# A first layer issued in another sequence, and a last output written out in two column halves

## The chip, the cores and the metric

The kernel runs on one core of a Trainium2 chip. The metric is device time in microseconds (us) of one execution; the median of three runs before the change is 726.11 us (725.8 to 727.15).

The engines are named as the profile names them: PE (TensorE, matrix products; PEld is its weight load), DVE (VectorE), ACT (ScalarE), POOL (GpSimd), SP (SyncE, which here only issues DMAs). SPq and ACTq are the sequencers of SP and ACT when they issue a DMA.

## The reference, cut to what matters

```python
def _attn_ref(q, k, v, alpha):            # (4, 8, 768, 48): a gated linear recurrence over time
    for t in range(S):
        state = alpha[:, :, t, :, None] * state + np.einsum('bhd,bhe->bhde', k[:, :, t], v[:, :, t])
        y[:, :, t] = np.einsum('bhd,bhde->bhe', q[:, :, t], state)

def _moe_ref(x, w_in, w_out, g_ln):       # first layer: x is (3072, 384), d_ff 1024
    h = x @ w_in
    solu = h * softmax(h)
    ln = (solu - mean(solu)) / sqrt(var(solu) + 1e-6) * g_ln
    return ln @ w_out

def _moe2_ref(x, w_in, w_out):            # second layer, d_ff 2048
    h = x @ w_in
    return (h * np.cos(h)) @ w_out
```

## The kernel before, in words

The work has two stages. The first stage does the recurrence and the first layer together, in 24 chunks of 128 tokens. The second stage does the second layer, in 6 blocks of 512 tokens by 16 chunks of the hidden dimension.

**The first stage.** A chunk i loads a pack (q, k and the decay alpha, 128 partitions) and v. DVE scans alpha forwards (`S1`, line 251), inverts the totals (`S3`) and scans backwards (`S4`, line 262). The scans scale q and k: the q product is `QP` on POOL or `QV` on DVE (line 276), the k product `KR` on POOL or `KV` on DVE (line 271). PE turns k (`TR`), ACT copies the result out (`KT`), PE makes scores (`SC`, line 295), DVE masks them (`MV`), PE makes the state (`ST`, line 346), DVE adds it up (`SD`, two halves), PE makes the values (`VA`, line 327). ACT and DVE split these into a high and a low part (`XH`, `XL`). Then come the hidden products of three k slices (`HD i.0` to `HD i.2`, line 395, 18 matmuls in all), DVE's maximum (`SM`, line 401), ACT's exponential (`EX`), the normalisation, turns (`TU`, `TH`, `TL`) and the projection (`PR`, `PX`).

**The weights.** They arrive as float64 bit patterns and are turned into float32 on the chip. For a block n: `CL` loads it (SP), `C1` shifts the upper word (DVE, line 183), `C2` and `CA` make the lower word on ACT (lines 190, 194), an integer add puts them together: `CD` on POOL or `CV` on DVE (line 198). `WH` copies the high part (ACT, line 212), and `WL` (POOL) or `WV` (DVE, line 218) subtracts the rest. Blocks 0 to 5 are `w_in` (512 columns each), 6 to 9 `w_out` (768 columns), 10 to 25 the second layer's, which `WS` stores to memory for later.

**The order.** Each engine works its queue strictly in order. `PLAN` is a text of 1104 words; the program walks it and issues one operation per word, so the sequence of words is the sequence of each engine's queue. `UN` is a matmul pair on constant data, with no use but to keep PE at work; five of them (`WARM`) stand ahead of the plan. `LP` and `LQ` load the decay part and the q and k part of a pack, `LV` loads v, `LD` all of it, and `ID` loads the identity, the mask and the norm's weights; `BP`, `BQ` and `BC` are the same loads issued by ACT.

**Buffers that set the order.** Line 459 and its like take PSUM tiles from one ring of three, tag `rot`: `TR` takes two, `TU` two, `ST`, `PR` and `UN` one each, and a new owner waits until the readers of the old one are done. Raw `w_in` blocks use two buffers for even and two for odd blocks, so the third even or odd load waits until the first is converted.

**The end.** `out_end` (line 626) copies the three output slices of a block from PSUM with a factor of 2 and stores each. For the last block, slice 0 is copied by ACT and stored by SP; slices 1 and 2 (`late`) are copied by DVE and stored by ACT's queue.

Of the kernel before, what the change touches and what calls it, by code (L numbers as in the profile page):

```python
# [79 lines left out]
NO3 TU2 C110 O24 O34 PR0.1 QV8 XL6 HD5.0 TH2.0 HD5.1 S48 A44 S19 KR8 TH2.1 TL2.1 TL2.0 C210 MV7 HD5.2 SA7 S39 TU3  # L80
PX0.1 TH3.0 SM5 TH3.1 EX5 VA7 TL3.0 TL3.1 O15 SC8 TR8 XH7 SQ4 PR1.0 O25 PA4 O35 PW4 HD6.0 KT8 PB4 XL7 S49 A45 HD6.1
CA10 NO4 HD6.2 TU4 CD10 MV8 VA8 PX1.0 SQ5 LD10 S110 QV9 TH4.0 TH4.1 SM6 EX6 TL4.0 CL11 ST8 C111 PR1.1 O16 O26 S310 O36
KV9 PA5 C211 PW5 S410 PB5 XH8 A46 SQ6 SD8 QV10 NO5 PA6 XL8 PX1.1 HD7.0 CL12 SP8 CA11 LD11 HD7.1 HD7.2 TL4.1 TR9 SC9
KT9 KV10 SM7 EX7 TR10 KT10 ST9 MV9 S111 VA9 SC10 A17 S311 TU5 SD9 PR1.2 O27 WS10 XH9 PW6 O37 TH5.0 HD8.0 XL9 CD11 QP11
C112 O47 S411 SP9 LD12 HD8.1 MV10 KV11 C212 TL5.0 S112 CL13 TH5.1 HD8.2 PB6 SQ7 TL5.1 PA7 CA12 PX1.2 NO6 VA10 SM8 EX8
ST10 SC11 QP12 CD12 WS11 CL14 TU6 SD10 C113 O18 PW7 PR2.0 S312 XH10 O28 SP10 C213 LD13 O38 WS12 S412 PB7 NO7 TH6.1
HD9.0 CA13 PX2.0 TH6.0 XL10 C114 HD9.1 HD9.2 CD13 KR12 TL6.0 O48 TL6.1 SQ8 SM9 PR2.2 CL15 MV11 EX9 TR12 A19 S113 PX2.2
KT12 SC12 S313 TU7 O29 VA11 PA8 O39 XH11 LD14 PR2.1 TH7.0 HD10.0 QV13 A49 PW8 MV12 TL7.0 HD10.1 XL11 S114 HD10.2 S413
S314 C214 TH7.1 PB8 TL7.1 SQ9 VA12 ST12 CA14 LD15 KR13 NO8 WS13 SM10 QV14 SD12 CV14 PX2.1 EX10 SC13 O110 TU8 TH8.0
PR3.0 XH12 O210 O310 TH8.1 S414 S115 HD11.0 WS14 KV14 XL12 PA9 PX3.0 C215 TL8.0 A410 HD11.1 MV13 SQ10 S315 PA10 HD11.2  # L90
PW9 TL8.1 PB9 PR3.2 TR13 CA15 KT13 VA13 PX3.2 ST13 TR14 SM11 NO9 S415 PW10 SC14 QP15 C115 KT14 SD13 XH13 SA13 XL13 TU9
MV14 CD15 TH9.0 TH9.1 EX11 TL9.0 CL16 PR3.1 TL9.1 C216 LD16 VA14 ST14 C116 KV15 S116 SD14 CA16 CL17 PX3.1 QP16 O111
SA14 O211 SC15 TR15 PR4.0 O311 XH14 CD16 WS15 HD12.0 HD12.1 C217 CA17 C117 S316 PB10 LD17 O411 HD12.2 SQ11 PA11 KT15
S117 PW11 S416 XL14 MV15 KR16 VA15 PX4.0 ST15 CL18 SM12 WS16 CV17 NO10 EX12 SD15 SC16 S317 SP15 TU10 O112 O212 PR4.1
# [853 lines left out]
```

## Time and profile before

| | |
|---|---|
| median of three runs | 726.11 us (725.8 to 727.15) |
| the profiled execution | 727.55 us |
| its span, first to last instruction | 725.7 us |
| PE busy | 708.5 us, 98% of the span |
| DVE, ACT, POOL busy | 81%, 60%, 17% |
| mean granted TensorE clock | 0.992 of full |

PE's busy share is not its share of peak: matmuls overlap, and at half clock the same matmul is busy twice as long. The span and the time of the profiled execution differ by 1.85 us, which lie outside the first and last instruction. The execution that was profiled was 1.4 us above the median.

### The profile page before, as it was taken

The numbers are of one execution on the slowest core, as the hardware profiler recorded it, in microseconds if no ns is written. First come the engines' busy times: TensorE is split into PE (matmuls) and PEld (weight loads), VectorE is DVE, ScalarE is ACT, GpSimd is POOL, SyncE is SP. The second block draws the span as 40 slices with busy tenths as digits, with TensorE's granted clock in tenths as the row PEclk, the third lists the DMA queues.
The fourth block names the chain that finished last, engine by engine and source line by source line (L and its number), as shares of the span: only waits on it lengthen the run. The fifth ranks groups of instructions, "written<-read, shape, count | busy, mean of one in ns | idle before, by whom it ended". The sixth has DMA issues, their size and how long they took to land.

```text
span 725.7 us, 14521 instructions
## 1 busy us (share of the span) xinstructions
PE 708.5 (98%) x5866; PEld 597.4 (82%) x5866; DVE 586.2 (81%) x995; ACT 432.2 (60%) x768; POOL 119.8 (17%) x113
## 2 busy tenths in 40 slices
...
GB/s 310 286 200 114 66 215 245 146 140 270 195 142 134 242 39 72 31 37 78 97 138 1 155 70 51 65 124 51 37 142 63 46 100 138 43 88 131 110 44 47
DMA packets 28010, 85.36 MB, mean 118 GB/s; under 512 B 3104, under 2 KB 6304, under 8 KB 27936
## 3 DMA queue, kind: packets, MB, share of 16 engines
...
q8 instruction: 48, 0.79, 0.5%
...
HBM read 73.33 MB, written 11.01 MB: 116 GB/s over the span
## 4 chain that ended last, share of the span: by engine, by line
PE 89%; DVE 6%; DMA 2%; ACT 1%; issue 1%; POOL 0%; SPq 0%; DVEq 0%; POOLq 0%
PE ph L395 12%; PE o L622 9%; PE o L624 9%; PE o L623 9%; PE h L577 9%; PE h L576 9%; PE h L575 9%; PE po L484 5%; PE po L485 4%; PE po L486 4%; PE px L327 4%; PE pa L295 3%; DMA pk<-pack 2%; PE pl L463 1%; DVE P L251 1%; DVE c L401 1%
## 5 line engine op out<-in xcount | busy, mean ns | idle before, releaser
L595 ACT ACTIVATE g<-r,consts 128x512 f32<-128x512 f32 x96 | 69.6, 725 | 98.8 <-DVE r L589 98.8
L582 ACT ACTIVATE n<-h,consts 128x512 int32<-128x512 f32 x96 | 66.1, 688 | 81.1 <-PE h L577 81.1
L622 PE MATMUL o<-gh,w2h 128*128 128x512 f32 x288 | 112.4, 390 | 0.0
L624 PE MATMUL o<-gl,w2h 128*128 128x512 f32 x288 | 112.2, 390 | 0.0
L577 PE MATMUL h<-x2h,w2l 128*128 128x512 f32 x288 | 112.2, 390 | 0.0
L576 PE MATMUL h<-x2l,w2h 128*128 128x512 f32 x288 | 112.2, 390 | 0.0
L623 PE MATMUL o<-gh,w2l 128*128 128x512 f32 x288 | 112.2, 390 | 0.0
L575 PE MATMUL h<-x2h,w2h 128*128 128x512 f32 x288 | 112.2, 389 | 0.0
L588 DVE SCALAR_TENSOR_TENSOR r<-n,h 128x512 f32<-128x512 int32 x96 | 66.0, 688 | 31.1 <-ACT n L582 30.6
L600 DVE TENSOR_TENSOR g<-g,h 128x512 f32<-128x512 f32 x96 | 66.1, 689 | 25.5 <-ACT g L595 25.4
L484 PE MATMUL po<-lth,wout_h 128*128 128x256 f32 x288 | 83.0, 288 | 1.9 <-DVE S L362 1.0
L485 PE MATMUL po<-ltl,wout_h 128*128 128x256 f32 x288 | 80.6, 280 | 0.0
L486 PE MATMUL po<-lth,wout_l 128*128 128x256 f32 x288 | 80.4, 279 | 0.0
L589 DVE SCALAR_TENSOR_TENSOR r<-n,r 128x512 f32<-128x512 int32 x96 | 67.4, 702 | 3.3
L610 DVE TENSOR_TENSOR gl<-g,gh 128x512 fp32r<-128x512 f32 x96 | 65.7, 684 | 0.8 <-ACT gh L605 0.8
L624 PEld LDWEIGHTS o<-gl,w2h 128*128 128x128 f32 x288 | 54.1, 188 | 11.3 <-DVE gl L610 0.2
L622 PEld LDWEIGHTS o<-gh,w2h 128*128 128x128 f32 x288 | 54.1, 188 | 11.2 <-ACT x2T L490 0.2
L623 PEld LDWEIGHTS o<-gh,w2l 128*128 128x128 f32 x288 | 54.1, 188 | 11.2
L577 PEld LDWEIGHTS h<-x2h,w2l 128*128 128x128 f32 x288 | 54.1, 188 | 11.2
L576 PEld LDWEIGHTS h<-x2l,w2h 128*128 128x128 f32 x288 | 54.1, 188 | 11.2
L575 PEld LDWEIGHTS h<-x2h,w2h 128*128 128x128 f32 x288 | 54.1, 188 | 11.1
L605 ACT ACTIVATE gh<-g 128x512 fp32r<-128x512 f32 x96 | 59.9, 624 | 1.1 <-DVE g L600 0.8
(114 smaller groups left out, 1363.3 us busy)
## 6 DMA issues: line engine op xcount, KB each, us to landing
...
```

The costliest lines, as they stand in the source:

```text
L395: PE.matmul(ph[:, n * 512:(n + 1) * 512], xs[:, k, :], w[:, k, n * 512:(n + 1) * 512], start=k == 0 and xs is xh and w is win_h, stop=k == ...
L484: PE.matmul(po, wout_h[:, k, fs], lh[:, k, :], start=k == 0, stop=False)
L485: PE.matmul(po, wout_h[:, k, fs], ll[:, k, :], start=False, stop=False)
L486: PE.matmul(po, wout_l[:, k, fs], lh[:, k, :], start=False, stop=k == NF1 - 1)
L575: PE.matmul(ph, wh[:, ks], xh[:, k, :], start=k == 0, stop=False)
L576: PE.matmul(ph, wh[:, ks], xl[:, k, :], start=False, stop=False)
L577: PE.matmul(ph, wl[:, ks], xh[:, k, :], start=False, stop=k == KT - 1)
L589: V.scalar_tensor_tensor(out=r, in0=n, scalar=-C2, in1=r, op0=ALU.mult, op1=ALU.add)
L595: A.activation(g, r, AF.Sin, bias=halfpi)
L622: PE.matmul(po, wh[:, fs], gh, start=c == 0, stop=False)
L623: PE.matmul(po, wl[:, fs], gh, start=False, stop=False)
L624: PE.matmul(po, wh[:, fs], gl, start=False, stop=c == NF2 - 1)
```

## The change

The plan has the same set of steps in another sequence, from its first word to its last, and some steps change their engine. `out_end` changes for the last block: slices 1 and 2 are stored by SP, and the last slice is copied and stored in two halves of 256 columns, the first by ACT (copy and store), the second by DVE (copy) and SP (store).

How the steps differ by kind, counted over the whole plan, before and after: loads issued by ACT 3 and 0; integer adds on POOL (`CD`) 18 and 10, on DVE (`CV`) 8 and 16; q products on POOL (`QP`) 9 and 17, on DVE (`QV`) 15 and 7; k products on POOL 15 and 14, on DVE 9 and 10; residues on POOL (`WL`) 4 and 3, on DVE (`WV`) 6 and 7; small mean steps on DVE (`O4`) 13 and 9, on ACT (`A4`) 11 and 15; `UN` 7 and 7.

```diff
 PLAN = """
-UN1 LP0 CL1 BP1 UN1 LP2 S10 BQ0 BC3 C21 CL0 CA1 C23 ID S30 CA3 C20 C11 S40 S11 CA0 CL2 S12 S31 LQ1 KV0 S41 C22 C13 C10
-UN1 CV3 C12 CV0 LV0 TR0 CL6 KT0 LQ2 QP0 SC0 UN1 ST0 MV0 CA2 SD0 WH0 WV0 S32 CL4 CD1 QV1 WH1 VA0 S42 C16 WH3 CL5 KR1
-XH0 C26 CA6 WV1 XL0 C24 SC1 UN1 TR1 C25 C14 CA4 UN1 CA5 MV1 C15 LV1 CV4 HD0.0 CD2 WH2 LD3 KT1 VA1 ST1 CV5 LV2 S13 WL3
-WH4 WV2 CL7 S33 WH5 WV4 WV5 KR2 CD6 S43 C17 TR2 CL8 WH6 QP2 C27 KR3 HD0.1 XH1 SD1 SP1 KT2 HD0.2 SC2 CA7 SM0 TR3 CD7
-ST2 XL1 EX0 MV2 WL6 A10 O20 KT3 LD4 C28 O30 A40 WH7 SQ0 VA2 PA0 SD2 S14 UN1 HD1.0 HD1.1 C18 S34 CA8 PW0 XH2 QV3 HD1.2
-S44 SC3 QP4 SM1 PB0 XL2 EX1 SP2 ST3 CL9 CD8 A11 MV3 VA3 NO0 O21 KR4 O31 XH3 LD5 C29 TU0 HD2.0 TH0.0 HD2.1 A41 SD3
...
+LP0 LP1 S10 CL1 LQ0 S11 CL0 C21 S30 LP2 C11 LQ1 LV0 S40 ID CL2 QV0 S31 KV0 S41 CA1 C20 CV1 CL5 S12 C22 C10 KV1 CL3 SC0
+WH1 S32 LQ2 CL6 CA0 C12 UN1 TR0 S42 CA2 MV0 CD0 KT0 C13 WV1 CV2 UN1 C25 CL7 WH0 LV1 CL4 UN1 QV1 C23 TR1 VA0 CA5 WH2
+ST0 KV2 SC1 C26 C15 C16 KT1 XH0 CD5 CA3 UN1 CD3 MV1 WV0 SD0 ST1 C24 WH3 XL0 CA4 LD3 WH5 C14 SD1 TR2 UN1 QP2 KT2 WV2
+CA6 WV3 CV4 VA1 HD0.0 HD0.1 WH4 S13 SA1 XH1 CV6 WV4 S33 C27 LV2 WV5 S43 HD0.2 CL8 WH6 SC2 SM0 EX0 KR3 XL1 TR3 WL6 ST2
+MV2 A10 CA7 VA2 O20 KT3 O30 UN1 A40 SQ0 LD4 QP3 S14 PA0 HD1.0 XH2 C17 S34 S44 HD1.1 XL2 PW0 HD1.2 SD2 CD7 UN1 SM1 SC3
+SP2 C18 PB0 MV3 NO0 C28 QP4 EX1 KR4 O11 CA8 ST3 O21 TU0 TH0.0 VA3 LD5 O31 WH7 SD3 O41 SQ1 PA1 TH0.1 CD8 HD2.0 TL0.0
...
 """
...
                 ob = pools["q3"].tile([128, BLK], F32, name=f"ob{b}_{f}", tag="ob", bufs=3)
+                dst = a["outT"][f * 128:(f + 1) * 128, b * BLK:(b + 1) * BLK]
                 late = b == NBLK - 1 and f > 0
+                cut = BLK // 2 if late and f == KT - 1 else 0
+                if cut:
+                    A.activation(ob[:, :cut], O[b][f][:, :cut], AF.Copy, scale=2.0)
+                    A.dma_start(dst[:, :cut], ob[:, :cut])
                 if late:
-                    V.tensor_scalar(ob, O[b][f], 2.0, None, ALU.mult)
+                    V.tensor_scalar(ob[:, cut:], O[b][f][:, cut:], 2.0, None, ALU.mult)
                 else:
                     A.activation(ob, O[b][f], AF.Copy, scale=2.0)
-                (A if late else SP).dma_start(a["outT"][f * 128:(f + 1) * 128, b * BLK:(b + 1) * BLK], ob)
+                SP.dma_start(dst[:, cut:], ob[:, cut:])
```

## Rows read from the trace of the kernel before

**Rows 1.** The page: busy time of each engine, its share, its instructions.

```profile
PE 708.5 (98%) x5866; PEld 597.4 (82%) x5866; DVE 586.2 (81%) x995; ACT 432.2 (60%) x768; POOL 119.8 (17%) x113
```

**Rows 2.** One stretch: PE, PEld, DVE, ACT, POOL busy; clock; DMA share; GB/s.

```profile
40.00:60.00 20.00, 19.54 (x306) 15.51 (x305) 19.05 (x30) 17.44 (x36) 12.19 (x10) 1.00 0.53 176
```

**Rows 3.** Waits of PE, whole span: total us, times, longest.

```profile
PE pkt L286 <- DVE pk L271: 3.3, 1, 3.3
PE pa L295 <- DVE pk L276: 2.3, 1, 2.3
PE po L484 <- DVE S L362: 1.0, 1, 1.0
PE pa L295 <- POOL pk L271: 0.4, 1, 0.4
```

**Rows 4.** DVE's timeline of the head: start, us, line, operation.

```profile
4.63 1.23 DVE L251 TENSOR_TENSOR_SCAN P<-pk,d1p 128x516 f32<-128x516 f32 x1 [3.10 <-DMA pk<-pack]
6.94 0.43 DVE L183 TENSOR_SCALAR magso<-rawi 128x512 int32<-128x512 int32 x1 [0.80 <-DMA rawi<-win]
7.29 1.23 DVE L262 TENSOR_TENSOR_SCAN R<-pk,d1r 128x516 f32<-128x516 f32 x1
8.43 2.15 DVE L251 TENSOR_TENSOR_SCAN P<-pk,d1p 128x516 f32<-128x516 f32 x1
12.73 0.66 DVE L271 TENSOR_TENSOR pk<-pk,R 128x512 f32<-128x512 f32 x1
14.77 1.40 DVE L183 TENSOR_SCALAR mage<-rawi 128x512 int32<-128x512 int32 x1
19.62 1.68 DVE L218 TENSOR_TENSOR win_l<-mage,win_h 128x512 fp32r<-128x512 f32 x1
35.65 1.22 DVE L401 TENSOR_REDUCE c<-ph 128x1 f32<-128x1024 f32 x1 [0.51 <-PE ph L395]
```

**Rows 5.** POOL's timeline of the head.

```profile
7.53 1.95 POOL L276 TENSOR_TENSOR pk<-pk,P 128x512 f32<-128x512 f32 x1 [5.46 <-DMA pk<-pack]
9.45 2.19 POOL L198 TENSOR_TENSOR magso<-magso,rawi 128x512 int32<-128x512 int32 x1
14.61 1.28 POOL L271 TENSOR_TENSOR pk<-pk,R 128x512 f32<-128x512 f32 x1 [2.96 <-DVE R L262]
```

**Rows 6.** Busy time in stretches of 2 us, columns as in rows 2.

```profile
12.00:14.00 2.00, 0.52 (x12) 0.55 (x14) 2.00 (x4) 0.82 (x3) 0.00 (x0) 1.00 1.05 427
14.00:16.00 2.00, 2.00 (x18) 1.20 (x16) 2.00 (x3) 1.28 (x3) 1.28 (x1) 0.70 0.99 407
16.00:18.00 2.00, 1.91 (x34) 0.84 (x32) 2.00 (x5) 0.26 (x1) 0.75 (x1) 0.50 0.06 25
18.00:20.00 2.00, 1.08 (x32) 0.81 (x32) 1.97 (x4) 1.41 (x3) 1.35 (x2) 0.94 0.55 129
20.00:22.00 2.00, 0.00 (x0) 0.00 (x0) 2.00 (x4) 1.95 (x3) 0.76 (x1) 0.91 0.98 395
28.00:30.00 2.00, 2.00 (x8) 1.17 (x6) 2.00 (x5) 0.79 (x2) 0.15 (x1) 0.88 0.82 341
```

**Rows 7.** The chain that ended last, in order of time: start, us, what.

```profile
39.73 1.06 PE warm L515 x2
63.50 1.67 PE px L327 x56
104.10 4.09 PE ph L395 x18
```

**Rows 8.** What SP's queue waited for, first 40 us.

```profile
SPq L177 <- DVE mage L198: 7.3, 1, 7.3
```

**Rows 9.** The end: timeline, landing of stores; ACT copies of 256 columns.

```profile
719.40 1.37 DVE L631 TENSOR_SCALAR ob<-o 128x512 f32<-128x512 f32 x2 [1.28 <-PE o L624]
...
DMA to landing us min/median/max: 3.0/3.0/3.1
...
L303 ACT ACTIVATE kt<-pkt 128x256 f32<-128x256 f32 x10 | 3.3, 377 | 3.2 <-PE pkt L286 3.2
```

More of the change, by code (lines that the diff above doesn't have):

```diff
@@ L80 @@
[L80 to L94, printed above, removed]
@@ new lines @@
+WV9 SQ2 PA2 CL10 EX3 TL1.1 LD8 S46 PW2 A13 O23 O33 A43 QP6 SQ3 PR0.0 S17 PR0.2 CL11 HD4.0 S37 KV6 PX0.2 PX0.0 HD4.1
+S47 S18 XH5 KV7 QV7 TR6 KT6 SC6 XL5 PB2 MV6 TR7 KT7 HD4.2 C210 SM4 NO2 ST6 VA6 SD6 EX4 ST7 XH6 SC7 SD7 A14 TU2 PA3 PW3
+LD9 TH2.1 TH2.0 S38 PR0.1 PB3 O24 O34 HD5.0 HD5.1 A44 TL2.1 NO3 S19 S48 TL2.0 KV8 HD5.2 SQ4 QP8 TU3 XL6 CA10 MV7 SM5
+PA4 TH3.0 TL3.0 VA7 PW4 C110 TH3.1 SC8 PX0.1 TL3.1 EX5 SP7 TR8 PR1.0 O15 MV8 O25 O35 PB4 XH7 LD10 HD6.0 CD10 HD6.1 XL7
+NO4 A45 C211 HD6.2 S39 QP9 S49 KV9 C111 CL12 CA11 KT8 SQ5 CD11 VA8 ST8 SM6 SC9 PA5 PW5 S110 SD8 CL13 EX6 PX1.0 XH8 TU4
@@ new lines @@
+EX9 WS13 S413 KT12 A19 XH11 SC12 TU7 O29 O39 TH7.1 LD14 XL11 PA8 PR2.1 KR13 TH7.0 HD10.0 S114 PW8 CA14 A49 CV14 S314
+TL7.1 PB8 HD10.1 TL7.0 PX2.1 HD10.2 MV12 VA12 S414 ST12 TR13 NO8 SC13 C215 SD12 SM10 LD15 KT13 TU8 CA15 TH8.0 MV13
+EX10 SQ9 XH12 PR3.0 C115 PA9 QP14 TL8.0 WS14 O110 TH8.1 CL16 O210 PR3.2 O310 PW9 TL8.1 PB9 CL17 A410 HD11.0 PX3.0 S115
+HD11.1 HD11.2 XL12 S315 C116 SQ10 VA13 KV14 CV15 PX3.2 SM11 WS15 NO9 C216 CA16 CL18 ST13 CD16 EX11 SD13 TR14 SC14 LD16
+MV14 KT14 TU9 A111 TH9.1 O211 O311 S415 TH9.0 XH13 C117 PR3.1 XL13 PA10 HD12.0 SP13 QP15 C217 HD12.1 WS16 VA14 CA17
@@ new lines @@
+TL9.0 A411 ST14 KR15 SQ11 S116 PX3.1 CV17 PW10 C218 TL9.1 SD14 S316 SC15 PB10 C118 PA11 LD17 XH14 MV15 TR15 PW11 NO10
+XL14 S416 PR4.0 QP16 HD12.2 KR16 SA14 CA18 SM12 CV18 KT15 PX4.0 VA15 EX12 ST15 SD15 SC16 TU10 SP15 O112 O212 O312
+PR4.1 HD13.0 TH10.0 TH10.1 S117 TL10.1 CL19 S317 LD18 A412 XH15 QP17 TL10.0 HD13.1 C219 HD13.2 PB11 S417 PX4.1 SQ12
+MV16 WS17 TR16 NO11 KT16 KR17 SC17 CA19 TU11 C119 TH11.0 PA12 XL15 S118 CD19 VA16 SM13 TL11.0 TH11.1 TL11.1 PW12 EX13
+WS18 ST16 A113 O213 PR5.1 CL20 O313 HD14.0 PB12 S318 C120 LD19 A413 NO12 SQ13 S418 PR4.2 MV17 HD14.1 QP18 HD14.2 XH16
@@ new lines @@
+PX4.2 SD16 PX5.1 TU12 C220 SP16 SM14 KR18 PR5.2 PA13 S119 EX14 PW13 TH12.1 XL16 VA17 PB13 TL12.1 TH12.0 O114 TL12.0
+O214 QP19 S319 O314 TR18 PX5.2 O414 NO13 KT18 SC18 TU13 TH13.0 XH17 TH13.1 MV18 SQ14 S419 TL13.1 HD15.0 CA20 HD15.1
+TL13.0 PA14 KR19 LD20 HD15.2 SC19 TR19 ST18 XL17 SM15 KT19 VA18 EX15 CV20 XH18 S120 WS19 A115 ST19 CL21 S320 PR6.1
+O215 LD21 PW14 O315 CL22 S420 KR20 HD16.0 XL18 SD18 C221 O415 MV19 SD19 HD16.1 C121 HD16.2 SM16 PR5.0 PB14 VA19 SQ15
+PA15 PX6.1 NO14 CA21 EX16 A116 QP20 TR20 S121 WS20 C122 PX5.0 SC20 S321 KT20 QV21 PW15 CV21 S421 TU14 LD22 O216 O316
@@ new lines @@
+TH14.0 CL23 C222 PR6.2 MV20 CA22 XH19 SP19 HD17.0 HD17.1 CV22 TL14.0 S122 PX6.2 S322 HD17.2 TH14.1 KR21 WS22 ST20
+TL14.1 TR21 PB15 SC21 SD20 XL19 NO15 KT21 TU15 SM17 VA20 EX17 MV21 A117 O217 PR6.0 O416 XH20 TH15.1 O317 SQ16 PX6.0
+TL15.1 PA16 XL20 HD18.0 PW16 A417 SQ17 WS21 HD18.1 HD18.2 TH15.0 S422 TL15.0 PB16 SM18 ST21 CL24 SP20 QP22 VA21 NO16
+EX18 KR22 PA17 XH21 SD21 TU16 LD23 C223 CA23 PR7.1 O118 PX7.1 O218 O318 PW17 TH16.0 O418 C123 TL16.0 TH16.1 SQ18
+TL16.1 HD19.0 PB17 CV23 C124 HD19.1 NO17 HD19.2 SC22 CL25 SA21 TU17 PA18 SM19 WS23 TH17.0 C224 PR7.0 S123 S323 PW18
@@ new lines @@
+TL17.0 EX19 S423 TH17.1 O119 TL17.1 CA24 O219 PB18 KV23 QV23 PR8.0 O319 A419 PR7.2 HD20.0 CV24 HD20.1 HD20.2 MV22 SQ19
+PX7.0 C225 CA25 NO18 SM20 PX8.0 XL21 PX7.2 PR8.1 TR22 EX20 C125 PX8.1 CV25 KT22 SC23 TU18 O120 VA22 WS25 O220 PA19
+ST22 O320 TH18.0 TL18.0 SD22 HD21.0 WS24 MV23 XH22 PW19 HD21.1 HD21.2 XL22 PB19 TH18.1 O420 NO19 SA22 VA23 TL18.1 SB
+WD0 SQ20 PA20 WD1 TU19 XA0 SM21 EX21 O121 TH19.1 PR8.2 PW20 O221 WD2 WA0 TH19.0 O321 TL19.0 XA2 PB20 TL19.1 XH23 XA1
+HD22.0 XL23 XS1 A421 XS0 SQ21 HD22.1 XS2 HD22.2 PR9.0 SM22 PA21 PW21 PX8.2 WG0 H20 PX9.0 NO20 EX22 WA1 TU20 TH20.1
```

37 lines of the change are left out of this document (11 added, 26 removed).

## The prediction, made before the change was run

> **What bounds the kernel now.** I read the page's first part, then the stretches, then PE's waits, then the timelines of the head and of the end. PE is busy for 98% of the span [rows 1], and the list of its waits is short [rows 3]: behind the first 40 us it runs with next to no gap (0.46 us is missing from 40 to 60 us [rows 2]). So the time is the start-up until PE has unbroken work, then a fixed amount of PE work, then the copies and stores behind the last matmul. A change of sequence can gain at the two ends only, and can lose anywhere.
>
> The head is bound by DVE. It starts with the first scan at 4.63 us and has idled 0.80 and 0.51 us when it takes up the first maximum at 35.65 us, which waits for the last of the first chunk's 18 hidden products [rows 4]. From there on PE is nearly gapless, so I use this moment as the mark: what the mark gains, the end gains, unless new waits give it back.
>
> DVE is slowed in the head by POOL. A scan takes 1.23 us, but 2.15 us where it begins while POOL's product of 7.53 us is under way; it ends 1.1 us after that product. A shift takes 0.43, but 1.40; an operation of two SBUF inputs 0.66, but 1.68 [rows 4]. The POOL operations in those places stretch likewise (1.95 and 2.19 against 1.28 [rows 5]). One holds the other for a whole instruction. Masks, state adds and the maximum, which read PSUM, show no such stretch. Six DVE instructions are held before the mark, by some 1.0 us each (0.92, 0.97 and 1.02 in the rows shown), 5.9 us together.
>
> Here a rule of the Trainium skill bears on the change. Its page "Advanced Engine Details and Errata", section VectorE Performance Modes, says that POOL and Vector instructions of the two-port mode block each other; the page "GPSIMD Engine Reference", section Key points, adds Vector instructions with two SBUF inputs. By the narrower wording only the two held shifts, 2 us, could be won back; by the wider one all 5.9 us. The held scan and the held residue of rows 4 decide for the wider one, and I go by it.
>
> **The change part by part.**
>
> *Work on DVE up to the mark.* Before: 31.0 us elapsed (4.63 to 35.65), less 1.3 idle, less 5.9 held, is 23.8 us. By the two plans, the new queue holds, up to the same maximum, three products more (KV1, KV2, QV0 against KV0, QV1 and POOL's share), one residue more, one add of 512 columns fewer, one add of 768 more and one shift of 768 fewer. At 0.60 each for the net three (0.66 [rows 4], less the 0.06 or so by which neighbours overlap) that is 1.8; the add of 768 for the shift of 768 is 1.5 times 0.66 less 1.5 times 0.43, 0.3. So 25.9 us.
>
> *Holds that stay.* Until the mark POOL has four operations that can hold DVE (CD0, CD5, CD3, QP2), where it had nine. By the order of the queues, CD0 falls beside the first mask, CD5 beside the second, CD3 beside the state adds and the low part of x: these read PSUM and aren't held. QP2 follows CD3 at once and meets a shift. I take one hold of 1.0 us; the bounds are 0 and 4.
>
> *First load.* All loads go through SP in sequence. Before, two decay packs were in flight on two queues, and the first scan started at 4.63. Half of those 0.53 MB at some 410 GB/s (rows 6, 12 to 16 us) is 0.6 us: the first scan starts at 4.0 us (bounds 3.7 and 4.7). The issuing of three more loads by SP costs SP under half a microsecond each and nobody waits for it, since the transfers keep the queue full.
>
> *A wait on SP.* The load CL3 takes the buffer of block 1, which is free when DVE has run CV1. Queued behind it on SP are LQ2, CL6, CL7, LV1, CL4 and LD3. By the sum CV1 is done at about 11 us, while some 2.3 us of transfers are still outstanding; such a wait cost SP 7.3 us before [rows 8] and left the engines nearly idle from 16 to 18 us, at 25 GB/s [rows 6]. Now the transfers run through: pack 3, which the fourth scan needs, has 8.5 MB in and before it, lands at about 24 us and is needed at about 27. I cost it at nothing; without that cover it costs one for one beyond 1 to 3 us.
>
> *DVE as a whole.* 4.0 + 25.9 + 1.0 held + 0.5 (the second mask waits for the second scores, which PE has later than DVE) = 31.4 us to the maximum, if PE is ready.
>
> *PE up to the mark.* The last warm-up before the first hidden product needs a ring buffer that held the second state, so it waits for SD1. Behind SD1, DVE has 6.2 us up to the maximum (four residues and an add 3.0, two scans 2.3, the 768 add 0.9), so SD1 ends at 25.2. Then PE has the pair (1.06), 56 matmuls of values (1.67) and 18 hidden ones (4.1) [rows 7]: 32.0 us. PE is last, by 0.6 us.
>
> *The clock.* This is at full clock. Before, the granted clock fell to half (1.2 of 2.4 GHz) twice: PE had worked 0.52 us of 12 to 14 before it fell at 14.8, and 1.08 of 18 to 20 and nothing of 20 to 22 around the second fall at 21.6. It was back at 18.2 and at 28.5 after nearly full work (the shares 0.70, 0.94, 0.91 and 0.88 of rows 6 give these times). So the low stretches lasted 3.4 and 6.9 us. Now PE waits for KT0 (some 2.4 us idle) and again for SD0 and SD1 (some 3 us with 0.4 of work), just ahead of the 6.8 us that count. I take one short low stretch over them: half of 3.4, 1.7 us more. The mark is then 33.7 us, against 35.65: 1.95 gained. Bounds: no low stretch, 32.0; the long one, 35.4.
>
> *One warm-up moves behind the mark.* Ahead of SC3 stands a pair that wasn't there; 1.06 us, less at most the 0.46 us of gaps it can fill [rows 2]: 0.6 lost (bounds 0 and 1.06).
>
> *The middle.* From the mark to the last chunk the set of PE's work is the same; DVE's and POOL's loads are within about 1 us per ten chunks of the old by count of steps. New waits can't be read off. Six waits of PE lie behind 60 us, 2.8 us together, the longest 1.0 [rows 3]. I take the same sum again; the bounds are none of them and twice as many, 2.8 us to either side.
>
> *The end.* Before, DVE copies slices 1 and 2 from 719.40 to 720.77, and the last store lands 3.0 us after its issue [rows 9]. Now slice 2's halves are copied side by side: ACT's 256 columns take about 0.38 [rows 9], DVE's about half of 0.69 and a fixed part, an estimate of 0.42. Both are done 0.3 us earlier, and each store moves half the bytes, on two queues: 0.1 more. Gain 0.4 (bounds: -0.1, if the two readers of one PSUM tile exclude each other, and 0.7). Separate columns of a tile are tracked apart here: the load into pack 0's q columns was issued before the scan of its decay columns, so DVE's half doesn't wait for ACT's store.
>
> **The sum.** 1.95 - 0.6 + 0 + 0.4 = 1.75 us, against the profiled execution's own 727.55 (span 725.7 and 1.85 around it): 725.8. The median stood 1.4 lower; the same gain puts it at 724.3 us.
>
> **The rivals.**
>
> - *The clock holds.* With each of PE's new idle times shorter than the 3.3 us before the first fall [rows 3], no low stretch may come over the hidden products: 1.7 more, 722.6.
> - *The long low stretch.* PE stays at half clock for 6.9 us as it did from 21.6: 3.4 instead of 1.7, 726.0. For it: the idle time around SD0 resembles the one before that fall. Against it: PE's work behind it is unbroken, and such work brought the clock back by 18.2.
> - *It doesn't do what it says*: the head is bound by landings, since one queue brings the data later. Only the end's gain is left, 725.7. Against it: SP's queue alone moved 395 GB/s from 20 to 22 us [rows 6].
> - *Slower.* From chunk 6 on the new plan gives POOL the q products (17 against 9 in all). One takes POOL 1.28 alone, DVE 0.66 [rows 4, 5], and it queues behind adds. Where PE comes to the scores within some 1 us of its product, PE waits; a wait of this kind was there once, 0.4 us [rows 3]. If half of the eight moved ones bite with the 1.0 us of the longest wait of rows 3, 4.0 us go: 728.4. It outweighs the head from two such waits on.
>
> **How the numbers follow.** Forecast 724.3 (one short low stretch, 723.5 to 725.2): 0.38. Clock holds, 722.6: 0.28. Long low stretch, 726.0: 0.12. Landings, 725.7: 0.04. Slower, about 728.4: 0.18. A measurement of this kernel can tell about 0.2%, 1.45 us, from no change; so faster means below 724.65. Of the forecast's 0.38, 0.28 lies below: faster 0.56, same 0.26 (0.10 + 0.12 + 0.04), slower 0.18. The range, with the middle's 2.8 us to either side of 724.3, is 721.5 to 727.1; it leaves out most of the slower case.
>
> **What would show it.** First scan near 4.0; one DVE scan, shift or residue held before the mark; first maximum at 32 to 35 us; the granted clock low once between 24 and 30; transfers without a gap until 24 us; PE's waits behind 60 us near 2.8 us; the last copy ending 0.3 us sooner after the last matmul. Wrong: a first maximum beyond 35 us, several holds, or waits on POOL products at line 295 of more than 2 us together.

## The result, and the profile after

The changed kernel takes 729.96 us (median of 13 runs, 726.94 to 732.56), the kernel before 726.44 in the 13 runs taken beside them: the ratio is 1.0051, interval 1.0033 to 1.0068. That is slower by 3.5 us, where 724.3 was forecast, and outside the range of 721.5 to 727.1. The profiled execution took 731.45 us, with a span of 729.7 against 725.7 before.

To see where the 4.0 us of the span came in, I cut both traces at the same two points: the mark of the prediction (start of the first maximum, line 401) and the end of the last matmul (line 624).

| | before | after | difference |
|---|---|---|---|
| start to mark | 35.65 | 35.95 | +0.30 |
| mark to end of last matmul | 684.39 | 687.45 | +3.06 |
| end of last matmul to end of span | 5.66 | 6.30 | +0.64 |

The largest loss is in the middle, where the prediction had 0.6 us for a warm-up pair and nothing for the rest; the head gained nothing where 1.95 was forecast, and the end lost instead of gaining.

The page first: busy time, share and instructions of each engine in the kernel after. PE and DVE do about what they did [rows 1]; ACT has 11 instructions more, the two added table loads below among them.

```profile
PE 709.8 (97%) x5866; PEld 598.3 (82%) x5866; DVE 581.2 (80%) x993; ACT 437.5 (60%) x779; POOL 108.3 (15%) x110
```

PE's waits in the kernel after (total us, times, longest). The long waits of rows 3 are gone, and others stand in their place.

```profile
PE warm L515 <- DVE S L362: 2.7, 1, 2.7
PE pl L463 <- ACT so L454: 2.2, 1, 2.2
PE po L485 <- DVE ltl L477: 1.1, 2, 0.8
```

**The middle.** The wait at line 463 lies near 313 us. ACT's timeline there, and PE's line behind it, in the kernel after (start, us, engine, line, operation, idle time before it and its releaser):

```profile
309.29 1.28 ACT L595 ACT_TABLE_LOAD   x1
310.59 0.72 ACT L595 ACTIVATE g<-r,consts 128x512 f32<-128x512 f32 x1
311.33 1.28 ACT L407 ACT_TABLE_LOAD   x1
312.62 1.11 ACT L407 ACTIVATE e<-ph,c 128x1024 f32<-128x1024 f32 x1
313.99 1.24 ACT L454 ACTIVATE so<-so,c 128x1024 f32<-128x1024 f32 x1
315.28 1.01 PE L463 MATMUL pl<-fixed,so 64*128 64x64 f32 x14 [2.23 <-ACT so L454]
```

Line 407 is the exponential of the first layer, line 595 the cosine of the second. The new plan issues the first cosine (`CS0`) directly before the last exponential (`EX23`). ACT loads a function table, does the cosine, loads the exponential's table again, does the last exponential, and loads the cosine's table once more for the rest. The same place in the kernel before:

```profile
305.10 1.12 ACT L407 ACTIVATE e<-ph,c 128x1024 f32<-128x1024 f32 x1
315.47 1.28 ACT L595 ACT_TABLE_LOAD   x1
```

There all exponentials are done when the one change of table comes (each kernel also loads a table in its first microseconds). Stretches of the kernel after around that place (columns as in rows 2):

```profile
300.00:350.00 50.00, 47.77 (x341) 42.90 (x338) 25.33 (x41) 33.28 (x58) 6.64 (x5) 0.97 0.15 48
310.00:315.00 5.00, 3.06 (x18) 2.35 (x16) 1.83 (x5) 4.96 (x7) 0.00 (x0) 1.00 0.08 30
315.00:320.00 5.00, 4.72 (x38) 4.60 (x39) 3.92 (x7) 4.34 (x10) 0.56 (x1) 0.66 0.01 3
```

From 310 to 315 us PE is busy for 3.06 of 5 us and ACT for 4.96; then the granted clock is 0.66 on average over the next 5 us, which is 3.4 us at half. At half clock PE gets through half as much (in this execution a warm-up pair took 2.08 us from 11.99 us on, at half clock, and 1.10 us at 27.22), so by estimate 1.7 us are lost on top of the wait of 2.2. Before, PE was busy for 49.26 of the 50 us from 300, at full clock.

**The head.** DVE's and PE's lines up to the mark, in the kernel after:

```profile
3.55 2.36 DVE L251 TENSOR_TENSOR_SCAN P<-pk,d1p 128x516 f32<-128x516 f32 x2 [2.02 <-DMA pk<-pack]
7.79 0.43 DVE L183 TENSOR_SCALAR magso<-rawi 128x512 int32<-128x512 int32 x1 [1.82 <-DMA rawi<-win]
24.86 1.43 DVE L183 TENSOR_SCALAR mage<-rawi 128x512 int32<-128x512 int32 x1 [0.30 <-DMA rawi<-win]
26.21 0.86 DVE L362 TENSOR_TENSOR S<-pst,S 64x256 f32<-64x256 f32 x2
27.22 1.10 PE L515 MATMUL warm<-d1p 128*128 128x512 f32 x2 [2.74 <-DVE S L362]
35.95 1.23 DVE L401 TENSOR_REDUCE c<-ph 128x1 f32<-128x1024 f32 x1 [2.55 <-PE ph L395]
```

The first scan starts 1.08 us sooner than before, but DVE then waits 1.82 us for the first weight block, and the shift of block 4 at 24.86 waits for its block too and is held by POOL (1.43 against 0.43). So the second state is ready at 27.07 us and not at 25.2. Stretches of 2 us of the kernel after show how slowly the first data came in (last column GB/s), and the low clock ahead of the mark:

```profile
4.00:6.00 2.00, 2.00 (x5) 0.91 (x4) 1.98 (x3) 0.00 (x0) 0.00 (x0) 1.00 0.89 277
6.00:8.00 2.00, 1.64 (x4) 0.38 (x2) 0.21 (x1) 0.21 (x1) 0.00 (x0) 1.00 0.94 310
8.00:10.00 2.00, 0.00 (x0) 0.00 (x0) 2.00 (x5) 1.19 (x2) 0.00 (x0) 1.00 1.02 383
28.00:30.00 2.00, 2.00 (x41) 1.76 (x44) 2.00 (x3) 1.71 (x4) 0.00 (x0) 0.63 0.30 41
30.00:32.00 2.00, 2.00 (x26) 1.52 (x19) 2.00 (x5) 1.42 (x5) 0.00 (x0) 0.52 0.81 288
```

Before, with ACT issuing three of the first loads, the same two stretches moved this much:

```profile
4.00:6.00 2.00, 2.00 (x5) 0.90 (x4) 1.27 (x2) 0.00 (x0) 0.00 (x0) 1.00 1.04 426
6.00:8.00 2.00, 2.00 (x6) 0.88 (x5) 1.20 (x3) 1.06 (x2) 0.47 (x1) 1.00 1.02 409
```

SP issued the first weight block (block 1) 0.47 us later than before, and DVE took it up 0.85 us later (7.79 against 6.94 us). The issue before, then after:

```profile
1.17 0.42 SPq L177 DMA_DIRECT2D rawi<-win  x1
1.64 0.42 SPq L177 DMA_DIRECT2D rawi<-win  x1
```

**The end.** The copies behind the last matmul in the kernel after, and SP's issues of the last stores (min, median and longest in ns):

```profile
722.75 0.69 DVE L636 TENSOR_SCALAR ob<-o 128x512 f32<-128x512 f32 x1 [1.28 <-PE o L624]
723.43 0.38 ACT L633 ACTIVATE ob<-o 128x256 f32<-128x256 f32 x1 [0.77 <-PE o L624]
723.85 0.42 DVE L636 TENSOR_SCALAR ob<-o 128x256 f32<-128x256 f32 x1 [0.40 <-ACT ob L633]
L639 SPq DMA_DIRECT2D outT<-ob x3: 343/751/1296, 722.7 to 724.8; - x3
```

DVE's half starts only when ACT's half is done, after an idle 0.40 us. Both take the predicted 0.38 and 0.42, but one after the other.

### The profile page after: what moved, and what is told of

The parts are those of the page before. It is cut to its first block, busy times and chain, and to the rows that moved or that the text cites. A ratio compares the mean times of both kernels' runs of the same rounds, so it can differ in the third digit from the quotient of the medians.

```text
span 729.7 us, 14519 instructions
## 1 busy us (share of the span) xinstructions
PE 709.8 (97%) x5866; PEld 598.3 (82%) x5866; DVE 581.2 (80%) x993; ACT 437.5 (60%) x779; POOL 108.3 (15%) x110
## 4 chain that ended last, share of the span: by engine, by line
PE 90%; DMA 3%; ACT 3%; DVE 1%; POOL 1%; SPq 1%; issue 0%; DVEq 0%
PE ph L395 13%; PE o L622 9%; PE o L624 9%; PE o L623 9%; PE h L577 9%; PE h L576 9%; PE h L575 9%; PE po L484 5%; PE po L485 4%; PE po L486 4%; PE px L327 4%; PE pa L295 2%; DMA rawi<-win 2%; PE pl L463 2%; PE pst L346 1%; DMA rawo<-wout 1%
## 5 line engine op out<-in xcount | busy, mean ns | idle before, releaser
L624 PEld LDWEIGHTS o<-gl,w2h 128*128 128x128 f32 x288 | 54.1, 188 | 11.4 <-DVE gl L610 0.2
```

The lines of the kernel that those rows point to most:

```text
L624: PE.matmul(po, wh[:, fs], gl, start=False, stop=c == NF2 - 1)
```

## Theories and experiments

My theory after reading the two traces: the middle's loss is the early cosine; the head's gain was eaten by loads that come late because one queue issues them all; the end loses because the two halves are copied in turn. The rivals: the middle's loss is something else in the new sequence, above all the q products moved to POOL (the prediction's own slower case); the head's new sequence is worse on its own account; the two halves wait for each other because they are written to one SBUF tile. Times are medians; each ratio is against the kernel before, run on the same chip, and kernels are compared by their ratios (0.001 is 0.73 us), since the kernel before itself took 726.1 to 726.9 us in the different groups of runs. "Mark" and "middle" are those of the table above, from one profiled execution each.

**1. The cosine moved back, in the new kernel.**

```diff
-RS0 PR9.1 WA2 SM23 H21 TH21.0 TH21.1 PB22 WG2 CS0 CM0 EX23 O123 PX9.1 TL21.0 O223 NO22 TL21.1 TU22 O323 TN1 TH22.0
+RS0 PR9.1 WA2 SM23 H21 TH21.0 TH21.1 PB22 WG2 EX23 O123 PX9.1 TL21.0 O223 NO22 TL21.1 TU22 O323 TN1 CS0 CM0 TH22.0
```

> The changed kernel with one edit: the first cosine chunk of the second layer (CS0, CM0) is issued after the last exponential of the first layer (EX23) and not before it. Theory A (two more table loads on ACT, 1.28 us each, hold EX23; PE waits 2.2 us for the turns of chunk 23 and falls to half clock for 3.4 us): the wait of PE at line 463 goes, one reload of the table is left instead of two, and the time falls by 2 to 4 us against the changed kernel, to about 727. Theory B (the middle's loss is spread over the chunks because POOL makes more q products): the wait moves elsewhere and the time falls by less than 1 us, to about 729.5.

Measured: 727.97 us, ratio 1.0014 (1.0001 to 1.0027), where the new kernel has 1.0051: 2.7 us less. The wait at line 463 isn't among the waits, and the middle is 684.51 us, 0.1 above that of the kernel before. ACT's last exponential and the one change of table, and the stretch, in this kernel:

```profile
309.28 1.12 ACT L407 ACTIVATE e<-ph,c 128x1024 f32<-128x1024 f32 x1
313.90 1.28 ACT L595 ACT_TABLE_LOAD   x1
300.00:350.00 50.00, 49.54 (x357) 44.13 (x352) 27.64 (x45) 32.49 (x59) 6.65 (x5) 1.00 0.18 56
```

Two words moved behind the last exponential take out most of the loss. 1.0 us against the kernel before stays (0.1 to 2.0).

**2. The early cosine alone, in the kernel before.**

```diff
-EX23 PW22 O123 PB22 NO22 PR9.2 WG1 TH21.1 O223 O323 TL21.1 O423 WA2 PR9.1 WD3 H21 WG2 SQ23 PA23 PX9.1 PX9.2 TU22
-TH22.1 PR10.0 TL22.1 TH22.0 TN1 CS0 PW23 H22 PB23 RS1 NO23 PX10.0 TL22.0 TU23 CS1 CM0 PR10.2 CM1 SH0 SL0 TH23.0 TH23.1
+CS0 EX23 PW22 O123 PB22 NO22 PR9.2 WG1 TH21.1 O223 O323 TL21.1 O423 WA2 PR9.1 WD3 H21 WG2 SQ23 PA23 PX9.1 PX9.2 TU22
+TH22.1 PR10.0 TL22.1 TH22.0 TN1 PW23 H22 PB23 RS1 NO23 PX10.0 TL22.0 TU23 CS1 CM0 PR10.2 CM1 SH0 SL0 TH23.0 TH23.1
```

> The kernel before with one step moved: the first cosine of the second layer (CS0) is issued ahead of the last exponential of the first layer (EX23). If this alone makes the changed kernel's loss in the middle: two table loads more on ACT (2.6 us in front of EX23 and behind it), PE waits 2 to 2.5 us at line 463, the clock falls for 3.4 us behind it, time +2 to +3.5 us against before. If the loss needs the rest of the new sequence: below +1 us.

Measured: 729.15 us, ratio 1.0041 (1.0024 to 1.0057): one word in another place costs about 3.0 us (1.7 to 4.1). ACT's three loads of a table, PE's wait and the stretch, in this kernel:

```profile
303.52 1.28 ACT L595 ACT_TABLE_LOAD   x1
306.55 1.28 ACT L407 ACT_TABLE_LOAD   x1
319.26 1.28 ACT L595 ACT_TABLE_LOAD   x1
PE pl L463 <- ACT x2T L490: 1.5, 1, 1.5
300.00:350.00 50.00, 47.68 (x332) 42.57 (x331) 25.80 (x39) 31.72 (x53) 7.02 (x5) 0.97 0.17 49
```

The pattern is that of the new kernel: PE waits at line 463 (1.5 us), loses 1.6 us of busy time in the stretch, and the granted clock is low for a while. Taken out of the one and put into the other, the early cosine explains the greater part of the loss.

**3. The new head alone.** The new sequence up to the last hidden product of the first chunk, then the old one; the old end.

```diff
 PLAN = """
-UN1 LP0 CL1 BP1 UN1 LP2 S10 BQ0 BC3 C21 CL0 CA1 C23 ID S30 CA3 C20 C11 S40 S11 CA0 CL2 S12 S31 LQ1 KV0 S41 C22 C13 C10
...
+LP0 LP1 S10 CL1 LQ0 S11 CL0 C21 S30 LP2 C11 LQ1 LV0 S40 ID CL2 QV0 S31 KV0 S41 CA1 C20 CV1 CL5 S12 C22 C10 KV1 CL3 SC0
...
+CA6 WV3 CV4 VA1 HD0.0 HD0.1 WH4 S13 SA1 XH1 CV6 WV4 S33 C27 LV2 WV5 S43 HD0.2 C17 CL8 WH6 KR3 SC2 CA7 SM0 TR3 CD7 ST2
...
```

> The kernel before with the changed plan's steps up to the first chunk's last hidden product (HD0.2), then the rest of the old plan in its order, and the old end. Theory A (the head gains nothing, the middle loses): first maximum at about 36.0 us, the last matmul at 720.3, time 0 to +0.5 us against before. Theory B (the head starts a loss that grows later, since other buffers and other queues are filled): +2 us or more.

Measured: 726.06 us, ratio 0.9989 (0.9974 to 1.0005): no difference that can be told. The mark in this kernel:

```profile
36.59 1.23 DVE L401 TENSOR_REDUCE c<-ph 128x1 f32<-128x1024 f32 x1 [2.09 <-PE ph L395]
```

It is the latest of all, so the head itself doesn't gain. The six profiled executions with the old head (before and runs 2, 4, 5, 9 and 10) have their marks at 35.07 to 35.65 us, the four with the new head and SP alone (after and runs 1, 3 and 8) at 35.95 to 36.59: the new head is the slower of the two. The middle, though, is 681.86 us, 2.5 shorter than before's, in one execution: three waits of PE behind the mark are gone, for state adds (1.0 and 0.4 us) and for a POOL product (0.4), 1.8 us together; the other 0.7 I can't place. The cut falls between two warm-up pairs that changed places, so this kernel holds six `UN` and that of run 4 holds eight, where the two full plans hold seven; a pair takes 1.1 us.

**4. The new rest alone.** The old sequence up to that point, the new one behind it; the old end.

```diff
...
-WH4 WV2 CL7 S33 WH5 WV4 WV5 KR2 CD6 S43 C17 TR2 CL8 WH6 QP2 C27 KR3 HD0.1 XH1 SD1 SP1 KT2 HD0.2 SC2 CA7 SM0 TR3 CD7
+WH4 WV2 CL7 S33 WH5 WV4 WV5 KR2 CD6 S43 C17 TR2 CL8 WH6 QP2 C27 KR3 HD0.1 XH1 SD1 SP1 KT2 HD0.2 SC2 SM0 EX0 XL1 TR3
...
```

> The kernel before with the old plan's steps up to the first chunk's last hidden product, then the rest of the changed plan in its order, with the old end. Theory A (the loss of the changed kernel lies in its middle, in the early cosine): first maximum at 35.6 us as before, PE waits about 2.2 us at line 463 near 310 us, time +2 to +3.5 us against before. Theory B (the loss comes from the head's side effects): within 1 us of before.

Measured: 729.66 us, ratio 1.0056 (1.004 to 1.0071): the whole loss is in the rest, of which its one pair more can be up to 1.1 us. PE's wait and the stretch in this kernel:

```profile
PE pl L463 <- ACT so L454: 2.2, 1, 2.2
300.00:350.00 50.00, 47.77 (x339) 42.45 (x338) 26.84 (x42) 33.59 (x57) 6.65 (x5) 1.00 0.18 53
```

The wait is the new kernel's, 2.2 us. The clock stayed up here, and the middle is 686.03 us, 1.6 above before's instead of 3.1: whether the clock falls behind this wait differs from one execution to another.

**5. The q products on POOL, in the kernel before.** Eleven words of chunks 3 to 22, of this kind:

```diff
-... A40 WH7 SQ0 VA2 PA0 SD2 S14 UN1 HD1.0 HD1.1 C18 S34 CA8 PW0 XH2 QV3 HD1.2
+... A40 WH7 SQ0 VA2 PA0 SD2 S14 UN1 HD1.0 HD1.1 C18 S34 CA8 PW0 XH2 QP3 HD1.2
...
```

> The kernel before with eleven q products of the chunks from 3 on moved from DVE to POOL, as in the changed plan. By the rival named ahead of the run (products on POOL are late for the scores): PE's waits at line 295 on POOL's product grow from 0.4 to 2 us or more, time +2 us or more. If POOL has the room: PE's waits unchanged within 1 us, time within 0.7 us of before.

Measured: 725.71 us, ratio 0.9993 (0.9982 to 1.0004). PE's one wait for a POOL q product:

```profile
PE pa L295 <- POOL pk L276: 0.5, 1, 0.5
```

These are the eleven products that the change moves to POOL (it takes three others off, 8 in all), and they cost nothing that can be told. The prediction's slower rival, 728.4, rested on these products; its mechanism is not the one.

**6. Three of the first loads issued by ACT, in the new kernel.**

```diff
-LP0 LP1 S10 CL1 LQ0 S11 CL0 C21 S30 LP2 C11 LQ1 LV0 S40 ID CL2 QV0 S31 KV0 S41 CA1 C20 CV1 CL5 S12 C22 C10 KV1 CL3 SC0
+LP0 BP1 S10 CL1 BQ0 S11 BC0 C21 S30 LP2 C11 LQ1 LV0 S40 ID CL2 QV0 S31 KV0 S41 CA1 C20 CV1 CL5 S12 C22 C10 KV1 CL3 SC0
```

> The changed kernel with three of its early loads (LP1, LQ0, CL0) issued by ACT in place of SP, in the same places of the plan. Theory A (one queue alone moves its first loads at 270 to 330 GB/s and so the first weight block lands at 7.8 us; two queues move 400 to 430): the transfers run above 400 GB/s from 4 to 8 us, the first weight block lands near 7 us or before, DVE's wait for it falls from 1.8 to under 1 us, first maximum 1 to 2 us earlier than 35.95. Theory B (the rate is that of the loads' shape, not of the queue): rate and first maximum unchanged within 0.5 us.

Measured: 729.22 us, ratio 1.0053 (1.0033 to 1.0072), which can't be told from the new kernel's. The trace of the head in this kernel:

```profile
4.00:6.00 2.00, 2.00 (x4) 0.72 (x3) 1.45 (x2) 0.00 (x0) 0.00 (x0) 1.00 1.03 420
6.00:8.00 2.00, 2.00 (x6) 0.71 (x4) 2.00 (x4) 1.30 (x2) 0.00 (x0) 1.00 1.04 418
4.55 2.36 DVE L251 TENSOR_TENSOR_SCAN P<-pk,d1p 128x516 f32<-128x516 f32 x2 [3.02 <-DMA pk<-pack]
24.18 0.43 DVE L183 TENSOR_SCALAR mage<-rawi 128x512 int32<-128x512 int32 x1 [1.40 <-DMA rawi<-win]
34.67 1.23 DVE L401 TENSOR_REDUCE c<-ph 128x1 f32<-128x1024 f32 x1 [2.95 <-PE ph L395]
```

The rate from 4 to 8 us is 420 GB/s again, the first scan a microsecond later (two packs share the way, as before), and the wait for the first weight block is gone. The mark comes 1.3 us sooner although the clock was low for 6.8 us ahead of it in this execution; in the time nothing of it is to be seen. Block 4 is still waited for, 1.40 us.

**7. The same three loads, with the new head and the old rest.** The edit of run 6, made in the kernel of run 3.

```diff
-LP0 LP1 S10 CL1 LQ0 S11 CL0 C21 S30 LP2 C11 LQ1 LV0 S40 ID CL2 QV0 S31 KV0 S41 CA1 C20 CV1 CL5 S12 C22 C10 KV1 CL3 SC0
+LP0 BP1 S10 CL1 BQ0 S11 BC0 C21 S30 LP2 C11 LQ1 LV0 S40 ID CL2 QV0 S31 KV0 S41 CA1 C20 CV1 CL5 S12 C22 C10 KV1 CL3 SC0
```

> The kernel with the changed head, the old rest and the old end, and the same three loads issued by ACT. If the queue sets the head's landings: first maximum at 34 to 35 us and 1 to 2 us less than the same kernel with one queue (726.06), about 724.5. If not: 726.

Measured: 725.05 us, ratio 0.9984 (0.9972 to 0.9996). The head in this kernel:

```profile
25.95 1.10 PE L515 MATMUL warm<-d1p 128*128 128x512 f32 x2 [1.52 <-DVE S L362]
33.05 1.23 DVE L401 TENSOR_REDUCE c<-ph 128x1 f32<-128x1024 f32 x1 [0.46 <-PE ph L395]
20.00:40.00 20.00, 16.05 (x242) 11.61 (x243) 17.56 (x30) 16.86 (x34) 8.25 (x6) 1.00 0.73 255
```

The clock never fell here, and the mark is at 33.05. From the last warm-up to the maximum it is 7.1 us: that is the prediction's path at full clock (6.8 us), begun 0.75 us later than forecast (25.2). The ratios of runs 3 and 7 differ by 0.0005, 0.4 us, and their intervals overlap: what the three loads on ACT give is shown by the marks alone, not by the times.

**8. The old end in the new kernel, and 9. the new end in the kernel before.** Run 8 takes this edit back, run 9 makes it.

```diff
+                dst = a["outT"][f * 128:(f + 1) * 128, b * BLK:(b + 1) * BLK]
+                cut = BLK // 2 if late and f == KT - 1 else 0
+                if cut:
+                    A.activation(ob[:, :cut], O[b][f][:, :cut], AF.Copy, scale=2.0)
+                    A.dma_start(dst[:, :cut], ob[:, :cut])
-                    V.tensor_scalar(ob, O[b][f], 2.0, None, ALU.mult)
+                    V.tensor_scalar(ob[:, cut:], O[b][f][:, cut:], 2.0, None, ALU.mult)
...
+                SP.dma_start(dst[:, cut:], ob[:, cut:])
```

Run 8:

> The changed kernel with the end of before: slice 1 and 2 of the last block copied whole by DVE and stored by ACT's queue. Theory A (the halves cost 0.66 us, because DVE's half waits for ACT's and SP's stores are issued slowly): from the end of the last matmul to the end of the span 5.6 us instead of 6.3, so 0.7 us less than the changed kernel. Theory B (the slow issue was a chance of one execution): no difference, within 0.2 us.

Run 9:

> The kernel before with the end of the changed one alone. Theory A: last matmul at 720.0 as before, the span ends 6.3 us behind it: +0.7 us against before. Theory B (as predicted): -0.4 us.

Measured: the new kernel with the old end 729.68 us, ratio 1.0041 (1.0028 to 1.0055); the old kernel with the new end 727.34 us, ratio 1.0005 (0.9995 to 1.0014). The new end is worth -0.4 to +1.0 us by run 9, so the forecast gain of 0.4 stands at the very edge of what is left. DVE's second copy and the last stores in run 9:

```profile
719.77 0.42 DVE L636 TENSOR_SCALAR ob<-o 128x256 f32<-128x256 f32 x1 [0.42 <-ACT ob L633]
L639 SPq DMA_DIRECT2D outT<-ob x3: 344/447/1141, 718.6 to 720.6; - x3
```

The wait between the two halves is there again, and one of SP's issues takes 1.1 us where the shortest takes 0.34. From the end of the last matmul to the end of the span run 8 took 6.1 us, neither the 5.6 nor the 6.3 of its two theories. Over all profiled executions the old end took 5.4 to 6.3 us (nine, mean 6.0) and the new one 6.2 to 6.6 (five, mean 6.4): some 0.4 us more, and the 0.64 of the first pair of profiles is partly the chance of two executions.

**10. The halves in two SBUF tiles.** Run 9, with ACT's half written to a tile of its own.

```diff
+                oc = pools["q3"].tile([128, BLK // 2], F32, name=f"oc{b}_{f}", tag="oc", bufs=1) if cut else ob
-                    A.activation(ob[:, :cut], O[b][f][:, :cut], AF.Copy, scale=2.0)
-                    A.dma_start(dst[:, :cut], ob[:, :cut])
+                    A.activation(oc[:, :cut], O[b][f][:, :cut], AF.Copy, scale=2.0)
+                    A.dma_start(dst[:, :cut], oc[:, :cut])
```

> The kernel before with the new end, but the first half of the last slice goes to an SBUF tile of its own. Theory A (DVE's half waits for ACT's half because both read the same PSUM tile): the 0.40 us wait of DVE stays. Theory B (it waits because both write the same SBUF tile): both halves start together, the copies end 0.4 us sooner after the last matmul, and the end is as long as before's or shorter.

Measured: 727.95 us, ratio 1.0021 (1.0006 to 1.0036). The two copies in this kernel:

```profile
719.31 0.38 ACT L634 ACTIVATE oc<-o 128x256 f32<-128x256 f32 x1 [0.77 <-PE o L624]
719.72 0.42 DVE L637 TENSOR_SCALAR ob<-o 128x256 f32<-128x256 f32 x1 [0.40 <-ACT oc L634]
```

The wait of 0.40 us stays, with nothing shared but the PSUM tile that both read. So it lies between the two readers of that tile. The profile puts it down to a signal from ACT's copy (a semaphore); whether the chip needs the wait, or the order built into the program alone sets it, no run shows. Giving the halves two PSUM tiles wasn't tried.

**11. All three repairs in the new kernel.** Runs 1, 6 and 8 together.

```diff
-LP0 LP1 S10 CL1 LQ0 S11 CL0 ...
+LP0 BP1 S10 CL1 BQ0 S11 BC0 ...
...
-RS0 PR9.1 WA2 SM23 H21 TH21.0 TH21.1 PB22 WG2 CS0 CM0 EX23 ...
+RS0 PR9.1 WA2 SM23 H21 TH21.0 TH21.1 PB22 WG2 EX23 ...
...
-                SP.dma_start(dst[:, cut:], ob[:, cut:])
+                (A if late else SP).dma_start(a["outT"][f * 128:(f + 1) * 128, b * BLK:(b + 1) * BLK], ob)
```

> The changed kernel with the three repairs together: cosine behind the last exponential, three early loads on ACT, the old end. If the three causes add up: about -2 (cosine), -0.7 (loads) and -0.4 (end) against the changed kernel's 730.0: 726.5 to 727. If they hide one another: 728 or more.

Measured: 727.5 us, ratio 1.0018 (1.0005 to 1.0031): 2.4 us under the new kernel, still over the old. It differs from run 7 in the sequence behind the first chunk alone, and run 7 has 0.9984; the two intervals don't meet. So the new rest costs some 2.5 us more than the old one behind the same head, even with its cosine in the right place (2.1 by the middles of the two profiled executions, 684.80 and 682.72). PE's wait and a stretch in this kernel:

```profile
PE po L485 <- DVE ltl L477: 1.1, 2, 0.8
40.00:100.00 60.00, 58.59 (x832) 49.65 (x834) 53.42 (x83) 44.06 (x85) 30.76 (x24) 1.00 0.46 153
```

The same 60 us were busy for 59.53 before, and in run 7. The waits for `ltl` (1.1 and, at line 484, 0.5 us) are new, but the old rest of run 7 has other waits in their place: from 40 to 350 us PE is idle for 2.55 us in run 11 and for 2.11 in run 7, 0.4 more. With the warm-up pair that stands behind the mark only in the new rest (1.1 us) that makes 1.5 us by estimate; the remaining microsecond stays open.

**12. A version from the parts that help.** Run 7 with the q products of run 5.

```diff
-XL1 EX0 MV2 WL6 A10 O20 KT3 LD4 C28 O30 A40 WH7 SQ0 VA2 PA0 SD2 S14 UN1 HD1.0 HD1.1 C18 S34 CA8 PW0 XH2 QV3 HD1.2 S44
+XL1 EX0 MV2 WL6 A10 O20 KT3 LD4 C28 O30 A40 WH7 SQ0 VA2 PA0 SD2 S14 UN1 HD1.0 HD1.1 C18 S34 CA8 PW0 XH2 QP3 HD1.2 S44
...
```

> The changed head with three loads on ACT, the old rest with the eleven q products on POOL, the old end: the two parts that gained, put together. If they add: first maximum at 33 to 35 us, time 1.5 to 2.5 us below before (724 to 725). If the second hides behind the first: as the kernel with the head alone, 1.2 us below before.

Measured: 724.62 us, ratio 0.9976 (0.9963 to 0.9989). The mark is at 34.01 us, the middle 682.0. It beats both kernels, the one before by 1.7 us (0.8 to 2.7): new head, three first loads on ACT, old rest with its q products on POOL, old end. Its interval and run 7's overlap, so what the q products add can't be told.

## Why the prediction was wrong, by its own steps

From the forecast gain of 1.75 us to the 4.0 by which the profiled span grew it is 5.75 us: 2.46 of them came in the middle with its warm-up pair, 2.25 in the head, 1.04 at the end. The first two would each have turned the gain into a loss alone.

**The middle, costed at 0: this step failed, and it is the largest error.** It compared engine loads and counts of steps and took PE's waits as they were, within 2.8 us. It didn't look at what ACT is asked to do in a row. The sum of the waits stayed within those bounds: PE's waits behind 60 us are 3.5 us in the new kernel, where 2.8 were forecast and 5.6 was the bound. But 2.2 of them stand in one place, the clock fell behind it, and for a clock in the middle the sum had no term. The order of `CS0` and `EX23` stands in the two plans, and the one change of table at 315.47 us stood in the trace of before, with its 1.28 us. The cost could have been worked out: two more loads of 1.28 us and a cosine of 0.72 put ahead of the last exponential, 3.3 us at most, at a place where PE has no other work to fall back on. Measured, it is about 3.0 us alone (run 2) and 2.7 when taken out (run 1). Part of this is not the loads but the clock that falls behind PE's wait (3.4 us at half, 1.7 lost, in the new kernel's profile and none in run 4's). With the cosine put right the new kernel was still 1.0 us slower than before (run 1), so the cosine is most of the loss and not all of it.

The Trainium skill has the rule against this change: its page "ScalarE: Activation LUTs", section Rules for kernel authors, says to group functions by table set and finish one set before switching, and to reckon about 2.7 us for each switch. The trace agrees with the rule, but not with the figure: its loads take 1.28 us each, and the next function starts within 0.02 us (309.29 + 1.28 = 310.57, against 310.59).

**"One warm-up moves behind the mark", 0.6 lost:** not measured by itself. Run 1's middle, which has that pair, is 0.1 us above the old one, but 1.8 and 2.65 us above those of runs 7 and 3 (682.72 and 681.86), the old rest behind the new head; how much of this is the pair isn't shown.

**First load, 4.0 us forecast (3.7 to 4.7): better than its bound, but the step failed in what follows from it.** The scan started at 3.55. What failed is the rate and the sentence that nobody waits for SP's issuing. The transfers moved 277 and 310 GB/s from 4 to 8 us, where the estimate took 410. Of the profiled executions, the new kernel and runs 1, 3 and 8, all with SP alone, moved 277 to 336 GB/s from 4 to 6 us and had their marks at 35.95 to 36.59; runs 6, 7, 11 and 12, with three of the loads on ACT, moved 420 to 425 and had their marks at 33.05 to 34.67. The two groups don't overlap. The six executions with the old head, in which ACT issues three first loads too, moved 418 to 426. And DVE does wait, 1.82 us, for a block that SP issued 0.47 us later than before. The issuing isn't the whole of it: by 3.0 us SP had issued five loads, 2.1 MB, and by 6 us only some 1.2 MB had moved, so the queue had work.

**A wait on SP, costed at nothing: half right.** The transfers did run on at 368 to 418 GB/s from 8 to 26 us, as forecast. But I worked out the landing of pack 3 alone, which the fourth scan needs at 27 us. Block 4, in the queue just ahead of it, is needed earlier, by the shift that stands directly before the second state add, and landed at 24.86 us (24.18 in run 6, with DVE idle for 1.40 us ahead of it). The rival "landings", given 0.04, was the case that came in the head. It is the head's failed step, with the rate: 1.95 us of gain forecast, 0.30 lost.

**DVE up to the mark.** The theory of holds held: by the plan few POOL operations were left, the one forecast hold came (the shift at 24.86, 1.43 us), and one more, of a shift at 17.25 (0.97 against 0.43). 25.2 us for the second state became 27.07: the waits for blocks add 1.82 and 0.30 and another 0.16 at 14.65 us, the second hold 0.5; the first scan came 0.45 sooner, and the 0.5 set aside for the second mask wasn't needed. That makes 27.0.

**The clock.** One short low stretch was forecast and came (28.5 to 31.9 us, stretches above). Another, from about 11.4 to 14.9 us, wasn't forecast; DVE was idle for 0.16 us in it. Neither is fixed: run 7 had no low stretch ahead of the mark and run 6 one of 6.8 us, all with nearly the same head. From the second state to the mark it was 8.9 us after, 7.25 in run 7, 9.3 in run 6; forecast were 8.5, 6.8 and 10.2 for the three cases.

**The end, 0.4 gained (-0.1 to 0.7): wrong value, and the bound chosen against was nearer.** The prediction named it: "if the two readers of one PSUM tile exclude each other". DVE's copy does wait for ACT's (run 10), and the gain was put at 0.4 with no row of two such copies side by side; its row on separate columns is of an SBUF tile and of a store, and says nothing of two readers of PSUM. The copies end 0.87 us after the last matmul, where they ended 0.73 after it. The remaining 0.5 us of the 0.64 in the profile lie behind the copies: SP's issues of 0.75 and 1.3 us, where the shortest takes 0.34. Why an issue takes that long there isn't settled. The timed runs don't resolve the end; the mean of the profiled executions, 0.4 us longer, is against the forecast gain.

**The rivals.** "Slower" gave 728.4 by way of q products on POOL; run 5 refutes that way, and the new kernel has no wait at line 295 behind 40 us. It would have been the right sign for the wrong reason. "It doesn't do what it says", 725.7, was right for the head and knew nothing of the middle.

**What stays open.** Why SP's queue alone is slow from 4 to 8 us, when it moves 383 to 418 GB/s from 8 to 14; the long issues of the last stores; whether the chip or the program's order makes the second copy wait; a microsecond of the 2.5 that the new rest costs beyond the cosine (runs 7 and 11), and 0.7 us of the shorter middle of run 3.
